# Sending four first-layer weight tiles behind the inputs of later pairs: attention with decay and a soft mixture of experts on one core

## The chip, the cores and the metric

The kernel runs on 1 core of one Trainium2 chip. The metric is the device time in microseconds (us) of one execution. In the tables and rows, PE is TensorE's matmul, PEld its weight load, DVE is VectorE, ACT is ScalarE, POOL is GpSimd and SP is SyncE, which here does nothing but issue the transfers (DMAs). The profile is of one execution; its clock starts at the first instruction.

## The reference

All data is float32. Attention with decay per head, in blocks of 64 positions, feeds a soft mixture of 8 experts with 4 slots each:

```python
# q, k, v: (4 batches, 8 heads, 768 positions, 64)
for b in range(nb):
    intra = einsum('bhic,bhjc->bhij', qb, kb) * Dmask      # lam ** (i - j), lower triangle
    intra = einsum('bhij,bhjd->bhid', intra, vb)
    inter = einsum('bhid,bhde->bhie', qb * lam_pow, kv_state)
    out[:, :, sl] = intra + inter
    kv_state = lam_block * kv_state + einsum('bhsd,bhse->bhde', kb * rev_pow, vb)
# x: the output as (3072 tokens, 512); phi: (512, 32 slots)
logits = x @ phi
slot_input = softmax over tokens(logits).T @ x              # 32 x 512
for e in range(8):                                          # w1: (8, 512, 1024), w2: (8, 1024, 512)
    slot_out[e] = maximum(slot_input[e] @ w1[e], 0) @ w2[e]
return softmax over slots(logits) @ slot_out                # 3072 x 512
```

The two weight arrays are 16.8 MB each, q, k and v together some 19 MB, the output 6.3 MB.

## The kernel before

**The pairs.** The sequence is cut into blocks of 128 positions, and two batches are worked on at a time, so there are 12 pairs, p = 0 to 11. Each pair needs three input tiles of 512 KB (k, q and v; two buffers of each). In turn p of the main loop PE computes, in this order: the part carried over from the state (`carried(p)`, matmuls a<-q,st), the part from within the block (`values(p)`, a<-at,v), the new state (`state(p)`, s<-v,kd), and then the scores of the next pair (`scores(p + 1)`, w<-q,k), after which come the logits of two pairs, the slots' sums and the transposes. Every engine keeps the order in which the program is written. DVE multiplies the scores by the mask (at<-w,mask) and updates the state (st).

**The weights.** Each layer's weights come as 32 tiles of 512 KB: w1t for the first layer, w2t for the second. 35 buffers (28 called slab, 7 called hold) take all 32 w1t tiles and the first 3 w2t tiles; the other w2t tiles go into buffers that come free as the main loop ends (those of k, q, v, kd, mask, at, xt, x) and, from there on, into slabs whose w1t tile has been used. The first layer (a<-w1t,e and w<-w1t,e) and the second (r<-w2t,hz and w<-w2t,hz) run behind the main loop, and use the tiles in the order in which they are sent for. The output is written as 24 pieces of 256 KB (y<-o), the first ten before the second layer's last part, the other 14 after it.

**The order of transfers.** All transfers are issued by SP in one order and go to one queue. SP issues a transfer as soon as the ones ahead of it have been issued and its own conditions hold: a free buffer, a PE instruction that it is kept behind, and the landing of the transfer eight places ahead of it. In turn p the inputs of pair p + 2 are sent for, k behind `carried(p)`, q behind `state(p)`, v behind `scores(p + 1)`. Between them `SENT[p]`, four numbers, says how many weight tiles are sent for at the four points of the turn: behind k, behind q, behind v, and at the end of the turn.

```python
def next_weights(p, point, at_):
    for _ in range(SENT.get(p, (0, 0, 0, 0))[point]):
        if early:
            behind(load_early(1), at_)
        elif run["spare"] < SPARE:
            run["spare"] += 1
            behind(load_late(bufs=NSLAB), at_)
```

`early` is the list of w1t tiles that are left; when it is empty, the 3 spare slabs take w2t tiles. Two w1t tiles are sent for ahead of the loop.

Of the kernel before, what the change touches and what calls it, by code (L numbers as in the profile page):

```python
# [33 lines left out]
LAST = (1, 0, 2)  # L34

SENT = {
    0: (1, 0, 1, 1), 1: (1, 0, 1, 1), 2: (1, 1, 1, 1), 3: (1, 0, 1, 1), 4: (1, 0, 1, 1), 5: (1, 1, 1, 1),
    6: (1, 1, 1, 1), 7: (1, 1, 1, 1), 8: (1, 0, 1, 1), 9: (1, 0, 1, 0),
}
NHOLD = 7  # L40

# [767 lines left out]
```

## Time and profile before

| | |
|---|---|
| median of 3 runs | 159.81 us (159.24 to 159.82) |
| the profiled execution's own time | 158.95 us |
| its span, first to last instruction | 157.1 us |
| PE busy | 142.7 us (91%) |
| DVE, ACT, POOL busy | 97.9, 50.9, 22.0 us |
| bytes moved | 59.14 MB, 376 GB/s over the span |

The span is 1.85 us less than the execution's own time; that rest lies ahead of the first instruction and behind the last one. PE's busy time says how long matmuls were under way, not that PE ran at its peak. The queue's share of busy time (99.2% on the page) counts transfers that are under way, so it is the GB/s, not the share, that tells how much was moved.

### The profile page before, as it was taken

What the parts mean: (1) busy time and instruction counts of PE and PEld (TensorE: products, weight loads), DVE (VectorE), ACT (ScalarE), POOL (GpSimd) and SP (SyncE); (2) the same over time, 40 slices, a digit from 0 to 9 for tenths busy, and PEclk for the clock granted to TensorE, in tenths of its full rate; (3) what the DMA queues carried; (4) which work ended last, traced back from release to release, by engine and by line L of the source; (5) the groups of instructions that cost most, each with busy time, mean ns of one, the idle gap of its engine ahead of it and who ended that gap; (6) DMA issues with size and microseconds to landing.
All of it is one profiled execution on the core that took longest, in us unless ns stands there. A gap on an engine that the chain in (4) does not pass through costs nothing.

```text
span 157.1 us, 5471 instructions
## 1 busy us (share of the span) xinstructions
PE 142.7 (91%) x2336; PEld 112.6 (72%) x2336; DVE 97.9 (62%) x209; ACT 50.9 (32%) x119; POOL 22.0 (14%) x35
## 2 busy tenths in 40 slices
PE   6999999999999999989999799999899999999500
PEld 6898999897897999887999679687333365756500
DVE  4699792768829473949376691955579971705800
ACT  3020225130550245021613036015037981604600
POOL 1003030303003000212030300300024840000000
PEclk9999999999999999999999999999999999999975
DMA  4999999999999999999999999899999999998995
GB/s 105 351 396 396 384 352 407 414 409 417 405 417 406 412 411 413 409 410 416 409 412 408 407 406 366 318 288 308 406 403 407 404 408 407 391 334 302 370 384 188
DMA packets 30424, 59.14 MB, mean 376 GB/s; under 512 B 2753, under 2 KB 8897, under 8 KB 30401
## 3 DMA queue, kind: packets, MB, share of 16 engines
q1 hardware_dynamic: 30400, 58.80, 99.2%
q8 instruction: 18, 0.29, 0.7%
q14 instruction: 6, 0.04, 0.1%
HBM read 52.50 MB, written 6.29 MB: 374 GB/s over the span
## 4 chain that ended last, share of the span: by engine, by line
PE 67%; DMA 21%; DVE 2%; SPq 2%; issue 1%; DVEq 0%; ACT 0%
PE a L52 26%; PE w L52 25%; DMA q<-qT 19%; PE r L52 10%; PE s L52 7%; SPq L52 2%; DMA y<-o 2%; DVE o L52 2%; DVEq L805 0%; DVE s L52 0%; ACT e L52 0%; DVE e L52 0%; DVEq L52 0%
## 5 line engine op out<-in xcount | busy, mean ns | idle before, releaser
L52 DVE TENSOR_TENSOR at<-w,mask 128x512 f32<-128x512 f32 x48 | 30.7, 681 | 6.9 <-PE w L52 6.7
L52 PE MATMUL w<-q,k 64*128 64x128 f32 x384 | 24.9, 278 | 2.5 <-DMA q<-qT 2.5
L52 PEld LDWEIGHTS w<-q,k 64*128 64x128 f32 x384 | 22.6, 188 | 4.1 <-issue 2.5
L52 POOL TENSOR_TENSOR q<-q,qpow 128x512 f32<-128x512 f32 x10 | 12.8, 1277 | 83.4 <-PE w L52 60.7
L52 PE MATMUL a<-at,v 128*64 128x128 f32 x384 | 23.6, 276 | 0.0
L52 ACT COPY xt<-a 128x512 f32<-128x512 f32 x23 | 12.4, 589 | 33.6 <-PE a L52 33.5
L52 PEld LDWEIGHTS a<-at,v 128*64 128x64 f32 x384 | 20.7, 137 | 2.1 <-issue 2.1
L52 DVE SCALAR_TENSOR_TENSOR st<-st,qpow,s 128x128 f32<-128x128 f32 x32 | 9.0, 343 | 16.9 <-PE s L52 16.9
L52 ACT COPY x<-a 128x512 f32<-128x512 f32 x12 | 6.9, 587 | 24.7 <-PE a L52 24.7
L52 DVE TENSOR_TENSOR kd<-w,mask 128x512 f32<-128x512 f32 x18 | 12.0, 683 | 1.4 <-PE w L52 1.2
L52 PE MATMUL a<-q,st 64*64 64x128 f32 x320 | 11.0, 275 | 0.0
L52 PE MATMUL s<-v,kd 128*64 128x64 f32 x320 | 11.0, 222 | 0.0
L52 PE MATMUL w<-ident,k 128*128 128x128 f32 x72 | 10.8, 279 | 0.0
L52 PEld LDWEIGHTS s<-v,kd 128*64 128x64 f32 x320 | 10.7, 138 | 0.0
L52 PEld LDWEIGHTS a<-q,st 64*64 64x64 f32 x320 | 8.6, 132 | 2.3 <-issue 1.5
L52 PEld LDWEIGHTS w<-ident,k 128*128 128x128 f32 x72 | 8.0, 140 | 1.0
L52 PE MATMUL a<-ident,xt 128*128 128x128 f32 x56 | 8.5, 280 | 0.0
L52 PEld LDWEIGHTS a<-ident,xt 128*128 128x128 f32 x56 | 6.1, 140 | 3.2 <-issue 3.1
L52 ACT CAST ct<-part 32x256 fp32r<-32x256 f32 x20 | 8.1, 402 | 0.3
L52 PE MATMUL a<-w1t,e 128*32 128x512 f32 x64 | 7.1, 594 | 0.4 <-DVE e L52 0.4
L52 PE MATMUL w<-w2t,hz 128*32 128x256 f32 x128 | 7.5, 380 | 0.0
L52 POOL CAST ct<-part 32x256 fp32r<-32x256 f32 x16 | 7.1, 445 | 2.7 <-issue 2.0
(118 smaller groups left out, 170.7 us busy)
## 6 DMA issues: line engine op xcount, KB each, us to landing
w1t<-w_x SPq DMA_DIRECT2D x32, 512.0 KB, 9.2
w2t<-w_x SPq DMA_DIRECT2D x32, 512.0 KB, 8.7
y<-o SPq DMA_DIRECT2D x24, 256.0 KB, 3.3
k<-kT SPq DMA_DIRECT2D x11, 512.0 KB, 7.6
q<-qT SPq DMA_DIRECT2D x11, 512.0 KB, 8.4
v<-vN SPq DMA_DIRECT2D x11, 512.0 KB, 8.9
k<-kT SPq DMA_DIRECT2D x2, 256.0 KB, 3.1
q<-qT SPq DMA_DIRECT2D x2, 256.0 KB, 3.5
```

The costliest lines, as they stand in the source:

```text
L52: return self._tc.keep_in_program_order(f(*args, **kwargs))
```

## The change

The numbers of `SENT` are changed, and nothing else. Four w1t tiles are no longer sent for in turns 0, 2, 5 and 7 (one each); turn 9 sends for two tiles at its end, and a new turn 10 for two behind `carried(10)` and `values(10)`.

```diff
 SENT = {
-    0: (1, 0, 1, 1), 1: (1, 0, 1, 1), 2: (1, 1, 1, 1), 3: (1, 0, 1, 1), 4: (1, 0, 1, 1), 5: (1, 1, 1, 1),
-    6: (1, 1, 1, 1), 7: (1, 1, 1, 1), 8: (1, 0, 1, 1), 9: (1, 0, 1, 0),
+    0: (1, 0, 0, 1), 1: (1, 0, 1, 1), 2: (1, 0, 1, 1), 3: (1, 0, 1, 1), 4: (1, 0, 1, 1), 5: (1, 0, 1, 1),
+    6: (1, 1, 1, 1), 7: (1, 0, 1, 1), 8: (1, 0, 1, 1), 9: (1, 0, 1, 2), 10: (2, 0, 0, 0),
 }
```

The sum of the numbers is 33 before and after (30 w1t tiles and 3 w2t tiles). The instructions of PE, DVE, ACT and POOL keep their order; SP's order alone changes. The first place is SP's order in turns 0 and 1, from v of pair 2 to v of pair 3, before:

```order
L52 DMA v_253<-vN 128x2x512
L52 DMA w1t_255<-w1_x 128x1024
L52 DMA w1t_267<-w1_x 128x1024
L52 DMA k_306<-kT 128x2x512
L52 DMA w1t_308<-w1_x 128x1024
L52 DMA q_333<-qT 128x2x512
L52 DMA v_357<-vN 128x2x512
```

And the same place after the change:

```order
L52 DMA v_253<-vN 128x2x512
L52 DMA w1t_265<-w1_x 128x1024
L52 DMA k_304<-kT 128x2x512
L52 DMA w1t_306<-w1_x 128x1024
L52 DMA q_331<-qT 128x2x512
L52 DMA v_355<-vN 128x2x512
```

One weight tile less stands ahead of pair 3's k, q and v, and ahead of all that follows. The same happens behind q of pair 4, of pair 7 and of pair 9, so that v of pair 4 has two tiles fewer ahead of it, v of pair 7 three, and v of pair 9 and all inputs of pairs 10 and 11 four.

The second place is SP's order at the end of the main loop, from the last tile of turn 8 on; k, q and v are those of pair 11. Before:

```order
L52 DMA w2t_1232<-w2_x 128x2x512
L52 DMA k_1266<-kT 128x2x512
L52 DMA w2t_1268<-w2_x 128x2x512
L52 DMA q_1293<-qT 128x2x512
L52 DMA v_1317<-vN 128x2x512
L52 DMA w2t_1319<-w2_x 128x2x512
L52 DMA w2t_1374<-w2_x 128x2x512
L52 DMA w2t_1392<-w2_x 128x2x512
L52 DMA w2t_1443<-w2_x 128x2x512
```

After the change:

```order
L52 DMA w1t_1224<-w1_x 128x1024
L52 DMA k_1258<-kT 128x2x512
L52 DMA w1t_1260<-w1_x 128x1024
L52 DMA q_1285<-qT 128x2x512
L52 DMA v_1309<-vN 128x2x512
L52 DMA w1t_1311<-w1_x 128x1024
L52 DMA w1t_1366<-w1_x 128x1024
L52 DMA w2t_1368<-w2_x 128x2x512
L52 DMA w2t_1370<-w2_x 128x2x512
L52 DMA w2t_1388<-w2_x 128x2x512
L52 DMA w2t_1416<-w2_x 128x2x512
L52 DMA w2t_1418<-w2_x 128x2x512
L52 DMA w2t_1443<-w2_x 128x2x512
```

The last two w1t tiles and all w2t tiles now stand behind pair 11's v, and four more tiles stand between that v and the w2t tile that goes into v's freed buffer (w2t_1443). From that tile on the order is the same, and the same set of tiles stands ahead of it.

## Rows read from the trace of the kernel before

**Rows 1.** The page: span, and all that the queue moved.

```profile
span 157.1 us, 5471 instructions
...
DMA packets 30424, 59.14 MB, mean 376 GB/s; under 512 B 2753, under 2 KB 8897, under 8 KB 30401
```

**Rows 2.** Groups on PE, 11.4 to 94.3 us: busy, mean ns, idle before <-releaser.

```profile
L52 PE MATMUL w<-q,k 64*128 64x128 f32 x320 | 20.6, 278 | 2.3 <-DMA q<-qT 2.2
L52 PE MATMUL a<-at,v 128*64 128x128 f32 x288 | 17.7, 276 | 0.0
```

**Rows 3.** PE's timeline: start, us, what, idle before <-releaser.

```profile
28.39 2.06 PE L52 MATMUL w<-q,k 64*128 64x128 f32 x32 [0.27 <-DMA q<-qT]
...
35.94 2.06 PE L52 MATMUL w<-q,k 64*128 64x128 f32 x32 [0.38 <-DMA q<-qT]
...
69.03 2.06 PE L52 MATMUL w<-q,k 64*128 64x128 f32 x32 [0.57 <-DMA q<-qT]
...
87.70 2.06 PE L52 MATMUL w<-q,k 64*128 64x128 f32 x32 [1.02 <-DMA q<-qT]
...
118.19 7.05 PE L52 MATMUL w<-w1t,e 128*32 128x512 f32 x64
...
136.68 5.82 PE L52 MATMUL w<-w2t,hz 128*32 128x256 f32 x104
```

**Rows 4.** The chain that ended last: start, us, what (issue to landing).

```profile
78.83 8.73 DMA q<-qT
```

**Rows 5.** Windows: PE, PEld, DVE, ACT, POOL busy (instructions), PEclk, DMA share, GB/s.

```profile
40.00:86.00 46.00, 45.40 (x827) 40.28 (x827) 29.53 (x60) 15.71 (x39) 5.11 (x4) 1.00 1.04 411
94.30:98.20 3.90, 3.90 (x98) 3.64 (x97) 0.53 (x3) 2.54 (x8) 0.00 (x0) 1.00 1.02 367
98.20:102.10 3.90, 3.90 (x48) 2.67 (x46) 3.58 (x8) 0.27 (x1) 1.28 (x1) 1.00 0.86 319
102.10:106.00 3.90, 3.90 (x85) 3.12 (x85) 2.05 (x4) 0.59 (x1) 0.00 (x0) 1.00 0.96 284
106.00:110.00 4.00, 3.75 (x57) 3.05 (x58) 2.20 (x7) 2.13 (x7) 0.00 (x0) 1.00 1.02 311
146.50:155.00 8.50, 1.10 (x9) 0.87 (x7) 2.34 (x4) 1.58 (x4) 0.00 (x0) 0.77 1.09 384
```

**Rows 6.** SP's timeline, six short windows: when single transfers were issued.

```profile
47.20 0.38 SPq L52 DMA_DIRECT2D v<-vN  x1
...
88.19 0.37 SPq L52 DMA_DIRECT2D v<-vN  x1
...
100.54 0.37 SPq L52 DMA_DIRECT2D w2t<-w_x  x1
...
102.83 0.37 SPq L52 DMA_DIRECT2D w2t<-w_x  x1
...
128.89 0.75 SPq L52 DMA_DIRECT2D w2t<-w_x  x1
...
152.24 0.58 SPq L52 DMA_DIRECT2D y<-o  x1
```

**Rows 7.** The same six transfers: KB, and us from issue to landing.

```profile
v<-vN SPq DMA_DIRECT2D x1, 512.0 KB, 6.6
...
v<-vN SPq DMA_DIRECT2D x1, 512.0 KB, 8.5
...
w2t<-w_x SPq DMA_DIRECT2D x1, 512.0 KB, 4.2
...
w2t<-w_x SPq DMA_DIRECT2D x1, 512.0 KB, 6.3
...
w2t<-w_x SPq DMA_DIRECT2D x1, 512.0 KB, 10.2
...
y<-o SPq DMA_DIRECT2D x1, 256.0 KB, 3.4
```

**Rows 8.** Tile w1t, all 32 transfers.

```profile
DMA to landing us min/median/max: 5.2/9.2/10.6
```

**Rows 9.** DVE's timeline behind the longest of PE's waits.

```profile
88.87 1.29 DVE L52 TENSOR_TENSOR at<-w,mask 128x512 f32<-128x512 f32 x2 [1.01 <-PE w L52]
```

## The prediction

> **What bounds the kernel now.** I read the page's totals first, then the groups on PE in the main loop, then PE's own timeline, and last the transfers one by one. The page gives a span of 157.1 us in which the one queue moved 59.14 MB [rows 1]. In the main loop PE is almost never idle: of all its groups there, only the scores stand behind a wait that counts, 2.3 us in all, and 2.2 of them ended when a q tile landed; the group below it, like all others, has 0.0 [rows 2]. The timeline shows where these waits are: 0.27 us ahead of pair 3's scores, 0.38 ahead of pair 4's, 0.57 ahead of pair 8's and 1.02 ahead of pair 10's [rows 3]. The chain of waits says the same from the other side: q of pair 10 is issued at 78.83 and lands 8.73 later, at 87.56, and the scores start at 87.70 [rows 3, 4]. So each late q was sent for in time, and then stood in the queue behind other tiles.
>
> The queue is the second thing to watch. From 40 to 86 us it moves 411 GB/s, so a tile of 512 KB (524,288 bytes) takes 1.28 us. From 94.3 to 110 us it moves only 367, 319, 284 and 311 GB/s [rows 5], since there the next tiles wait for buffers that PE and DVE still use. The time lost there against 411 GB/s is 3.9 x (1 - 367/411) = 0.42, then 0.87, 1.21 and, over 4.0 us, 0.97: 3.47 us. At the very end the last writes move at 384 GB/s, 0.68 us for each 256 KB [rows 5].
>
> **What the change removes.** From pair 3 on, inputs have fewer weight tiles ahead of them: one for q of pairs 3 and 4, three for q of pair 8, four for q of pair 10. In a queue that never runs dry that brings them forward by 1.28, 1.28, 3.8 and 5.1 us. PE needs them earlier by the wait itself and by what it has gained before: 0.27, then 0.38 + 0.27 = 0.65, then 1.22, then 2.24 us. Each is less than what the tile gains, so all four waits should go, and with 0.6 us or more to spare. Inputs that were in time before gain at least as many tiles, so none of them should become late. The sum of the four, 0.27 + 0.38 + 0.57 + 1.02, is **2.24 us**.
>
> Two things could keep part of it. First, the queue must not run dry: the shortest stay from issue to landing near the end of the loop, when little is queued, is 4.2 us (the transfer issued at 100.54) [rows 6, 7]. V of pair 6 now stays 6.6 us [rows 7]; with two tiles fewer ahead and issued 0.65 us earlier, that is 6.6 - 2.55 + 0.65 = 4.7. V of pair 11 stays 8.5 us [rows 7] and will stay 8.5 - 5.1 + 2.24 = 5.6. Both are above 4.2, so the queue gets short but stays filled. Second, DVE used PE's wait to catch up: behind the longest one it stood idle for 1.01 us, up to 88.87, until the scores came [rows 9]. So DVE was free from 87.86. Without the wait PE would start at 86.68 and be through the first half of the scores, which DVE waits for, 1.03 us later (half of 2.06, [rows 3]), at 87.71. DVE would then begin at most 0.15 us late, which at four places is 0.6 us if PE felt all of it; I take 0, since PE goes on to logits that do not need DVE's product, and keep 0.6 for the range.
>
> **What the change adds.** Four tiles, 5.1 us of the queue, move into the stretch with 3.47 us lost. Two w1t tiles are sent for behind all inputs; a w1t tile never took more than 10.6 us to land [rows 8], so they are there by about 101 us (my estimate: issue by 90). They are the last of the first layer and are used in the last quarter of the matmuls that start at 118.19 and take 7.05 us [rows 3], at 123.5. That costs nothing. What matters is whether w2t and the writes behind them come later, since all of them share the queue.
>
> Up to the transfer issued at 100.54 the same set of tiles has been sent for before and after. Before, it landed at 100.54 + 4.2 = 104.74 [rows 6, 7]. After: v of pair 11 landed at 88.19 + 8.5 = 96.69 and will land 5.1 us earlier, at 91.59; ten tiles then follow (six before), and 91.59 + 10 x 1.28 gives 104.4. The next transfer, issued at 102.83, landed at 102.83 + 6.3 = 109.13, which is 4.39 us behind the one ahead of it instead of 1.28 [rows 6, 7]: it goes into the mask's buffer, it was issued late, and the queue was nearly empty. After the change it is issued 2.24 us earlier, while the queue still has tiles to move. If only the issue counts, it lands at 106.9; if only the queue counts, at 105.7. So the stream of w2t tiles comes 2.2 to 3.4 us earlier, and I take 2.24.
>
> Is that enough? The last w2t tile landed at 128.89 + 10.2 = 139.09 [rows 6, 7]. PE's last part, 104 instructions of 0.056 us from 136.68 [rows 3], first touches it some 92 instructions in, at 141.8: 2.7 us to spare, so PE may run 2.24 us ahead even if that tile came no earlier. The writes are tighter. 24 of them at 0.68 us need 16.4 us; behind 139.09 that is 155.5, and the last one landed at 152.24 + 3.4 = 155.64 [rows 6, 7]. There is only 0.2 us between the two: to let the end come 2.24 us earlier, the stream has to come at least 2.0 us earlier too. The estimate above, 2.2 to 3.4, meets that with little room. The sum therefore stays at 2.24 us: the span goes from 157.1 to 154.9, the profiled execution from 158.95 to 156.7. The median of the runs shown, 159.81, lies 0.86 us above the profiled execution; taken off the median the sum gives 157.6. Should those 0.86 us be waits of the same kind, they go as well, and 156.7 is the low bound. I say 157.5.
>
> **The rivals.** The first is that the stream, not PE, sets the end. If the slow transfer at 102.83 takes its 4.39 us again although the queue is full, it lands at 104.4 + 4.39 = 108.8, the stream gains 0.4 us, and the end gains that and the 0.2 from above: 0.6 us, 159.2. For it speaks that the transfers there were slow while some were under way (DMA share 0.96 at 284 GB/s, [rows 5]); against it, that this coincides with late issues.
>
> A stronger form is that the queue bounds the whole program; since the bytes stay the same, nothing would change: 159.8. Against it stand the 3.47 us lost in four windows. The Trainium skill's "Perfetto Trace Analysis", section "Identifying the Most-Contended Engine", says to work on the most contended engine and to judge DMA by how far HBM's bandwidth is used; its section "Engine Utilization" puts a core's full share at 358 GB/s. By that figure an estimate for 59.14 MB is 165 us, more than the span, the kernel would have no slack and a new order of the same bytes would bring nothing. The trace does not agree: the core alone moved 411 GB/s for 46 us.
>
> The second rival ends slower. If the queue runs dry in the loop, once it has lost its backlog, the four tiles come on top: 5.1 us of work against at most 3.47 us of gaps leaves the stream 1.6 us late. The last w2t tile would land at 140.7, still in time for PE, but the writes would end at 140.7 + 16.4 = 157.1 instead of 155.64: 1.5 us slower, 161.3. It decides from the point where the stream is over 0.2 us late at 139.09, and becomes visible from 1.0 us. For it speaks that v of pair 6 gets within 0.5 us of the shortest stay; against it, that v of pair 11 keeps 1.4.
>
> The third is that waits merely shrink, by DVE's 0.15 us at each place or by engines of the queue that lag: 0.6 us of the gain lost, 158.2. I count it with the forecast.
>
> **How the numbers follow.** About 0.5% (0.8 us) is what a measurement of this kernel can tell from no change. Chances: the forecast with its own range of 156.7 to 158.3, 0.74; the stream late by the slow transfer, 159.2, 0.13; no change because the queue bounds all, 0.05; slower, 161.3, 0.08. Most of the second case lies within 0.5%, some of it above. So faster 0.79, same 0.14, slower 0.07. The range runs from 156.6, just below the low bound, to 159.2, so that it takes in the second case and leaves out the last two and the edges.
>
> **What would show it.** Right: no scores behind a q tile from 11 to 94 us in PE's groups; stays from issue to landing of 4 to 6 us for inputs from pair 9 on; the first layer's matmuls some 2.2 us earlier; more GB/s in the 16 us behind 92 us; the last w2t tile down by 2 us or more. Wrong: waits of PE for another input or for DVE's product; a queue below 400 GB/s ahead of 90 us; the last w2t tile at 139 or later while PE's last part is earlier, and writes that then follow each other at 0.68 us.

## The result and the profile after

The changed kernel takes 157.79 us (median of 4 runs, 156.70 to 158.92) against 159.81 (159.24 to 159.90): a ratio of 0.9883, 95% interval 0.9841 to 0.9925. Timed again beside three other kernels it took 157.76 (157.43 to 158.39) against 159.56, ratio 0.9887 (0.9846 to 0.9928). So it is faster by about 1.8 to 2.0 us.

The profiled execution took 158.19 us, with a span of 156.3 us, which is only 0.8 us less than before. It is worth reading closely, because it holds both what was gained and what was lost. First the same groups on PE as in [rows 2], in the same stretch (busy, mean ns, idle before):

```profile
L52 PE MATMUL w<-q,k 64*128 64x128 f32 x320 | 20.6, 278 | 0.5 <-DMA q<-qT 0.4
L52 PE MATMUL a<-at,v 128*64 128x128 f32 x306 | 18.9, 276 | 0.0
```

Of 2.3 us of waiting ahead of the scores 0.5 is left. PE's timeline has one wait for q where [rows 3] had four, and the marks behind it are the first layer's start and the first matmul behind the output's second split:

```profile
18.37 2.06 PE L52 MATMUL w<-q,k 64*128 64x128 f32 x32
...
68.09 2.06 PE L52 MATMUL w<-q,k 64*128 64x128 f32 x32 [0.45 <-DMA q<-qT]
...
109.21 1.92 PE L52 MATMUL a<-w1t,e 128*32 128x512 f32 x16 [0.44 <-DVE e L52]
...
142.35 0.74 PE L52 MATMUL a<-s,ct 128*128 128x256 f32 x4 [0.21 <-DVE s L52]
```

The same marks in the kernel before:

```profile
18.43 2.06 PE L52 MATMUL w<-q,k 64*128 64x128 f32 x32
...
111.24 1.92 PE L52 MATMUL a<-w1t,e 128*32 128x512 f32 x16 [0.44 <-DVE e L52]
...
144.38 0.74 PE L52 MATMUL a<-s,ct 128*128 128x256 f32 x4 [0.21 <-DVE s L52]
```

PE is 2.03 us earlier at both later marks, and yet the span lost only 0.8. The windows show where the queue worked (columns as in [rows 5]):

```profile
40.00:86.00 46.00, 45.46 (x840) 40.33 (x840) 28.92 (x60) 15.78 (x39) 5.10 (x4) 1.00 1.01 391
94.30:98.20 3.90, 3.90 (x84) 3.71 (x79) 1.71 (x5) 1.34 (x3) 0.45 (x1) 1.00 1.01 380
98.20:102.10 3.90, 3.90 (x69) 2.60 (x67) 3.23 (x6) 0.00 (x0) 0.83 (x1) 1.00 1.05 408
102.10:106.00 3.90, 3.90 (x63) 2.92 (x58) 1.37 (x4) 1.55 (x4) 0.00 (x0) 1.00 1.05 402
106.00:110.00 4.00, 3.31 (x58) 2.23 (x61) 2.69 (x9) 1.16 (x5) 0.00 (x0) 1.00 1.05 406
...
40.00:58.00 18.00, 18.00 (x314) 15.68 (x314) 11.17 (x24) 6.98 (x17) 1.28 (x1) 1.00 0.97 367
```

The lean windows behind 94 us are filled, as forecast: 380, 408, 402 and 406 GB/s in place of 367, 319, 284 and 311. But a new lean stretch stands in the main loop, 367 GB/s from 40 to 58 us, where PE is busy all the time. Single transfers, first as issued by SP (start, us): v of pair 6 and the weight tile behind it, v of pair 11, the counterpart of the slow transfer issued at 102.83 before [rows 6], the last w2t tile and the last write.

```profile
46.36 0.38 SPq L52 DMA_DIRECT2D v<-vN  x1
...
47.25 0.34 SPq L52 DMA_DIRECT2D w1t<-w_x  x1
...
86.19 0.38 SPq L52 DMA_DIRECT2D v<-vN  x1
...
100.80 0.37 SPq L52 DMA_DIRECT2D w2t<-w_x  x1
...
128.24 0.75 SPq L52 DMA_DIRECT2D w2t<-w_x  x1
...
150.30 0.56 SPq L52 DMA_DIRECT2D y<-o  x1
```

And the same six with the time from issue to landing in the last column:

```profile
v<-vN SPq DMA_DIRECT2D x1, 512.0 KB, 4.6
...
w1t<-w_x SPq DMA_DIRECT2D x1, 512.0 KB, 6.6
...
v<-vN SPq DMA_DIRECT2D x1, 512.0 KB, 7.1
...
w2t<-w_x SPq DMA_DIRECT2D x1, 512.0 KB, 6.9
...
w2t<-w_x SPq DMA_DIRECT2D x1, 512.0 KB, 10.2
...
y<-o SPq DMA_DIRECT2D x1, 256.0 KB, 4.6
```

V of pair 6 stays 4.6 us in the queue (6.6 before, [rows 7]) and lands at 51.0; the weight tile right behind it lands at 53.9, so this tile took 2.9 us of the queue instead of 1.28. The last w2t tile lands at 138.4, 0.6 us earlier than before, not 2. The 24 writes need 16.4 us behind it, which gives 154.8, and the last one lands at 154.9: here the stream, not PE, sets the end.

### The profile page after: what moved, and what is told of

It reads as the page before. It is cut to its first block, busy times and chain, and to the rows that moved or that the text cites. A ratio compares the mean times of both kernels' runs of the same rounds, so it can differ in the third digit from the quotient of the medians.

```text
span 156.3 us, 5474 instructions
## 1 busy us (share of the span) xinstructions
PE 142.7 (91%) x2336; PEld 112.8 (72%) x2336; DVE 97.6 (62%) x209; ACT 50.9 (33%) x119; POOL 22.0 (14%) x35
## 4 chain that ended last, share of the span: by engine, by line
PE 84%; DMA 5%; DVE 2%; issue 1%; DVEq 0%; ACT 0%
PE w L52 33%; PE a L52 30%; PE s L52 12%; PE r L52 10%; DMA q<-qT 5%; DVE o L52 1%; DVEq L805 0%; DVE s L52 0%; DVE warm L52 0%; ACT so L52 0%; ACT e L52 0%; DVE e L52 0%; DVE so L52 0%; DVEq L52 0%
```

## Experiments

The theory: the gain is that inputs land earlier because fewer weight tiles stand ahead of them, and the end is the later of two times, PE's and the stream's. The main rival: the gain comes from filling the lean windows behind 94 us. In each, only what the diff shows is changed; SP's order alone moves, unless it says otherwise.

**One tile, turn 0 alone.**

```diff
-    0: (1, 0, 1, 1),  ...  9: (1, 0, 1, 0),
+    0: (1, 0, 0, 1),  ...  9: (1, 0, 1, 1),
```

> One tile only leaves its place (turn 0) and is sent for in turn 9, so every later input has one tile, 1.28 us, less ahead of it. If the gain is that inputs land earlier (my theory): the waits at pairs 3, 4 and 8 (0.27, 0.38, 0.57) go, at pair 10 about 0.96 us is left (2.24 needed, 1.28 given), gain 1.28 us against the kernel before, 158.5. If the gain comes from the four tiles filling the lean windows behind 94 us (rival), one tile gives a quarter of the 2.0 measured: 0.5 us, 159.3.

Measured: 157.98 us, ratio 0.9914 (0.9880 to 0.9947), 1.4 us faster. This fits the theory's 1.28 us; a quarter of the gain, 0.5 us, lies outside the interval. The profiled execution, with 159.12 us one of the slower ones of 12, shows the waits that stay, at pairs 8 and 10:

```profile
69.00 2.06 PE L52 MATMUL w<-q,k 64*128 64x128 f32 x32 [0.64 <-DMA q<-qT]
...
87.90 2.06 PE L52 MATMUL w<-q,k 64*128 64x128 f32 x32 [1.25 <-DMA q<-qT]
```

Pairs 3 and 4 wait no more, as expected; pair 8 still waits, which I had not expected, and pair 10 waits 1.25 instead of 0.96. This execution lies 1.1 us above the median, and in it PE gained only 0.6 us from pair 2's scores to the first layer, so the 1.4 us rests on the medians and not on this trace. One tile ahead of pair 10's q, issued at 76.08, landed 2.5 us behind the tile before it (82.8 to 85.3) instead of 1.28. Such delays differ from one execution to the next: the kernel of the third experiment below, whose transfers have the same order as before up to the last four w2t tiles, waits 0.20 us ahead of pair 4, 0.91 ahead of pair 8, 1.04 ahead of pair 10 and not at all ahead of pair 3, where [rows 3] have 0.38, 0.57, 1.02 and 0.27.

**Two tiles, turns 5 and 7 alone.**

```diff
-    5: (1, 1, 1, 1),  ...  7: (1, 1, 1, 1),  ...  9: (1, 0, 1, 0),
+    5: (1, 0, 1, 1),  ...  7: (1, 0, 1, 1),  ...  9: (1, 0, 1, 2),
```

> Two tiles leave their places (turns 5 and 7). My theory: the waits at pairs 3 and 4 (0.27 and 0.38) stay, those at pairs 8 and 10 (0.57 and 1.02) go, since one and two tiles give 1.28 and 2.55 us; gain 1.6 us, 158.2; and the queue keeps its length from 40 to 58 us, where the changed kernel's ran short, so that the last w2t tile should land earlier than the changed kernel's 138.45. Rival (tiles fill the lean windows): half of the gain, 1.0 us, 158.8.

Measured: 157.53 us, ratio 0.9871 (0.9825 to 0.9918): 1.9 to 2.1 us faster, as much as the four tiles gave. The rival's 1.0 us lies outside the interval, the theory's 1.6 inside. The waits at pairs 3 and 4 stay, and those at pairs 8 and 10 are gone:

```profile
28.78 2.06 PE L52 MATMUL w<-q,k 64*128 64x128 f32 x32 [0.69 <-DMA q<-qT]
...
36.79 2.06 PE L52 MATMUL w<-q,k 64*128 64x128 f32 x32 [0.84 <-DMA q<-qT]
```

Both are longer in this execution than before (0.27 and 0.38), so a wait of one profile is not a fixed size. The queue keeps its rate from 40 to 58 us, 410 GB/s, since nothing was taken out ahead of that stretch, and the last w2t tile lands at 126.44 + 10.3 = 136.7. PE is later than in the changed kernel, the stream earlier, and the sum is no worse.

**The stream shortened at its end, in the kernel before and in the changed one.**

```diff
         Q, f, i = late.pop()
+        if len(late) < 4:
+            for y in range(2):
+                wt["w2", Q, 2 * i + y, f] = wt["w2", 1, y, 5]
+            return None
```

> The kernel before, without the transfers of the last four w2t tiles (the second layer's last part uses one earlier tile in their place, so the output's last part is not the reference's); PE's work is the same. The stream is 5.1 us shorter. If PE sets the end of the kernel before, as I read it, it stays within 0.4 us of it: 159.4 to 159.8. If the stream sets it, up to 5 us faster.

> The changed kernel without the transfers of the last four w2t tiles (same omission). If the stream sets the end of the changed kernel, as its profile reads (writes back to back from 138.45 on), it is faster than the changed kernel by what PE is ahead, 0.5 to 1.5 us, so 2.2 to 2.6 us faster than before in all: 156.5 to 157.3, with less spread from run to run. If PE alone sets the end, it equals the changed kernel, 157.8.

Measured: before, 159.42 us against 159.45, ratio 0.9994 (0.9966 to 1.0023); changed, 156.96 us, ratio 0.9834 (0.9790 to 0.9877), from 156.71 to 157.47. Taking 5.1 us of transfers away does nothing for the kernel before: PE sets its end. A stream that comes earlier can therefore not have been the gain, as the rival would have it. In the changed kernel the same omission brings the time from 157.8 to 157.0, with a range of 0.8 us instead of 2.2 and 1.0. The two intervals overlap, so the 0.8 us by itself is not certain; that the writes of the changed kernel's profile end where the stream's sum says, and not where PE's does, is the firmer sign. The changed kernel's profile without the four tiles has no wait for q behind the start, and its rate from 40 to 58 us is 384 GB/s.

**Only the order within a turn.**

```diff
-    0: (1, 0, 1, 1), 1: (1, 0, 1, 1), 2: (1, 1, 1, 1),  ...  9: (1, 0, 1, 0),
+    0: (0, 0, 2, 1), 1: (0, 0, 2, 1), 2: (0, 0, 3, 1),  ...  9: (0, 0, 2, 0),
```

> No tile leaves its turn: the weight tiles of a turn that stood behind k or q are sent for behind v, so that each q has one tile, 1.28 us, less of its own turn's weights ahead of it and the queue keeps its length. My theory (a q that lands earlier is the gain): as in the run that moves turn 0's tile alone, gain 1.3 us, 158.2. Rival (the tiles must leave the main loop): no change, 159.5.

Measured: 158.75 us, ratio 0.9929 (0.9896 to 0.9962). It is a gain of 0.8 to 1.1 us, less than the 1.3 expected (the interval reaches from 0.6 to 1.7), but no tile left the main loop, so the rival is wrong that the tiles must leave it. The profiled execution waits 0.62 us for pair 10's q, and in the main loop for no other.

**Three tiles, so that the queue keeps one more from turn 2 on.**

```diff
-    2: (1, 0, 1, 1),  ...  10: (2, 0, 0, 0),
+    2: (1, 1, 1, 1),  ...  10: (1, 0, 0, 0),
```

(The lines taken away are those of the changed kernel.)

> Three tiles leave their places (turns 0, 5 and 7); turn 2 keeps its fourth, so that the queue from 40 to 58 us is a tile longer than in the changed kernel, where the transfers ran thin and the stream lost time. My theory (both PE's waits and the stream matter): no q wait of over 0.3 us, the stream at 400 GB/s or more from 40 to 58 us, the last w2t tile below 138, 157.2, some 0.5 us faster than the changed kernel. Rival (the order of the stream has no part in the end): as the changed kernel, 157.8.

Measured: 157.34 us (156.54 to 158.05), ratio 0.9847 (0.9807 to 0.9888). It beats the kernel before, and stands 0.4 us below the changed one, which the intervals do not separate. The spans set them further apart: 154.3 to 155.8 us here against 155.6 to 156.5 for the changed kernel timed beside it, medians 155.05 and 155.9. The executions with three, with two and with eight tiles are each 2.2 to 2.3 us longer than their spans, those of all other kernels 1.8 to 1.9; what the 0.4 us outside the span are, no run shows. The profile with three tiles has the lowest span of all, 154.3 us, and no wait for q at all behind the start. The window from 40 to 58 us:

```profile
40.00:58.00 18.00, 18.00 (x312) 15.68 (x312) 11.34 (x24) 6.98 (x17) 1.27 (x1) 1.00 1.03 403
```

403 GB/s where the changed kernel had 367, with one tile more in the queue; the last w2t tile lands at 125.93 + 10.2 = 136.1. PE's marks:

```profile
18.58 2.06 PE L52 MATMUL w<-q,k 64*128 64x128 f32 x32
...
108.78 1.92 PE L52 MATMUL a<-w1t,e 128*32 128x512 f32 x16 [0.44 <-DVE e L52]
...
141.92 0.74 PE L52 MATMUL a<-s,ct 128*128 128x256 f32 x4 [0.21 <-DVE s L52]
```

**Eight tiles** (the lines taken away are again those of the changed kernel).

```diff
-    0: (1, 0, 0, 1), 1: (1, 0, 1, 1), 2: (1, 0, 1, 1),  ...  5: (1, 0, 1, 1),  ...  7: (1, 0, 1, 1),  ...  10: (2, 0, 0, 0),
+    0: (1, 0, 0, 1), 1: (1, 0, 0, 1), 2: (1, 0, 0, 1),  ...  5: (1, 0, 0, 1),  ...  7: (1, 0, 0, 1),  ...  10: (6, 0, 0, 0),
```

> Eight tiles leave the main loop instead of four. My theory: PE has no q waits left to lose, the queue runs dry within the loop (below 390 GB/s from 40 to 86 us), and the stream comes late: the last w2t tile at 142 or later, and the writes behind it end 16.4 us later; 161 to 163, slower than before. Rival (more tiles behind the inputs are better, the lean windows behind 94 us take them): 157 to 158.

Measured: 162.25 us, ratio 1.0161 (1.0123 to 1.0199), slower, as the theory says and near its number. The rate from 40 to 58 us (361 GB/s from 40 to 86), then PE's waits for transfers (us in total, times, longest), those for w2t in the second layer, that for q ahead of pair 1's scores:

```profile
40.00:58.00 18.00, 18.00 (x312) 15.69 (x311) 11.37 (x23) 6.94 (x16) 1.28 (x1) 1.00 0.94 347
```

```profile
PE w L52 <- DMA w2t<-w_x: 2.1, 4, 0.7
...
PE w L52 <- DMA q<-qT: 0.2, 1, 0.2
```

The last w2t tile lands at 132.47 + 10.5 = 143.0; 16.4 us more make 159.4, and the last write lands at 153.98 + 5.36 = 159.3.

**The changed kernel again.**

> The changed kernel once more, on the same chip as the three others. 157.8 (156.7 to 158.9). If the loss of the stream from 47 to 58 us in its first profile comes from the short queue, it is there again (below 390 GB/s from 40 to 58 us); if it was a chance event, the stream moves 405 GB/s or more there.

Measured: 157.76 us, as above. The lean stretch is there again, while no q is waited for behind the start:

```profile
40.00:58.00 18.00, 18.00 (x311) 15.85 (x310) 11.37 (x23) 6.65 (x16) 1.28 (x1) 1.00 1.01 374
```

And PE's marks:

```profile
19.06 2.06 PE L52 MATMUL w<-q,k 64*128 64x128 f32 x32
...
109.26 1.92 PE L52 MATMUL a<-w1t,e 128*32 128x512 f32 x16 [0.45 <-DVE e L52]
...
142.39 0.74 PE L52 MATMUL a<-s,ct 128*128 128x256 f32 x4 [0.21 <-DVE s L52]
```

## Why the prediction was right, and where a step failed

The time was forecast as 157.5 us and is 157.8. Two terms were off, PE's gain too small and the stream's too large, and they nearly cancel; that the time came within 0.3 us is in part luck. Of the signs of being wrong that were named ahead one came true, a queue below 400 GB/s ahead of 90 us (391 from 40 to 86 us); and of the signs of being right the stays of 4 to 6 us were missed (v of pair 11 stayed 7.1 us in the first profile and 6.2 in the second).

**What bounds the kernel before: right.** PE sets its end and the queue does not; with 5.1 us fewer transfers it took the same time. This also speaks against the stronger form of the first rival, in which the queue bounds everything. The 358 GB/s in the Trainium skill, "Perfetto Trace Analysis", section "Engine Utilization", was no bound here: the core moved 411 GB/s. The same section says that 358 is the share of a core when both cores of a pair use the memory, and that one core alone can go to some 120% of it; the trace agrees, with 115%. The estimate of 165 us left that condition out.

**The four waits: right, but mis-sized.** They go when the q tiles have fewer weight tiles ahead of them: one tile moved gave 1.4 us, and the new order within a turn a part. All four are gone in the changed kernel's second profile, while the first keeps 0.45 us ahead of pair 8. The term was 2.24 us, the sum of four idle times. From pair 2's scores to the first layer PE took 111.24 - 18.43 = 92.81 us before; in the changed kernel's second profile 109.26 - 19.06 = 90.20, and with three tiles moved 108.78 - 18.58 = 90.20 as well. So without the waits PE was 2.61 us earlier. PE's timeline counts a wait from the modelled end of the last matmul to the next start; the starts themselves lie further apart than that. Pair 10's scores start 87.70 - 79.52 = 8.18 us behind pair 9's before and 85.67 - 78.58 = 7.09 after, 1.09 for a wait of 1.02. The four places make 2.5 us in this way; the last 0.1 lies between pairs 5 and 6, where no q was waited for.

**"The queue gets short but stays filled": failed.** The stay of v of pair 6 came out as worked out, 4.6 for 4.7 us. But the sign was badly chosen: a stay above 4.2 us does not mean that the queue moves all it can. The transfer that stayed 4.2 us belongs to a stretch with 319 and 284 GB/s [rows 5, 6, 7], and it was not the shortest either, since the one issued at 98.30 stayed 4.0. What goes with the rate is the number of tiles under way. The fewest tiles that were issued and had not landed at any moment from 44 to 50 us, and the rate of these 6 us, in all ten profiles:

| fewest tiles under way | profiles | GB/s |
|---|---|---|
| 5 | before; before without four w2t tiles | 411, 411 |
| 4 | one tile; two; three; order within a turn | 396, 413, 398, 401 |
| 3 | changed; changed again; changed without four w2t tiles | 346, 313, 349 |
| 2 | eight tiles | 304 |

The rate from 40 to 58 us follows the number of tiles taken out ahead of pair 6's v: none, 410 GB/s (two tiles moved, in turns 5 and 7); one, 402 and 403 (turn 0 alone; three tiles); two, 367, 374 and 384 (the changed kernel twice, and without four w2t tiles); four, 347 (eight tiles). The tile that took 2.9 us in the first profile is not the cause: in the second it landed 1.2 us behind pair 6's v, and the stretch was lean all the same. Why three tiles under way do not fill the queue is not settled. The second rival, a queue that runs dry in the loop, so had the mechanism right, but with four tiles the loss was smaller than what PE gained; with eight it came out as that rival said.

**The stream 2.2 to 3.4 us earlier: failed.** Most of it follows from the step before: from 40 to 58 us the first profile lost 18 x (1 - 367/411) = 1.9 us of the stream. V of pair 11 landed at 86.19 + 7.1 = 93.3 and not at 91.59. The slow transfer that the first rival feared did not come back, since its counterpart, issued at 100.80, landed 1.3 us behind the tile ahead of it, with 402 to 408 GB/s around it. But it landed at 107.7, 2.0 us later than the 105.7 that the queue's sum gave, and so 1.4 earlier than before. One tile issued at 104.14 then landed 2.6 us behind the one ahead (111.6 to 114.2), for a reason that no run shows. The last w2t tile came at 138.4 in the first profile and at 127.47 + 10.2 = 137.7 in the second, so 0.6 and 1.4 us earlier, less than the 2.0 that the prediction had asked for. So the first rival named the right end, the stream, and the wrong place.

**The end as the later of two times: right.** The stream's sum is the landing of the last w2t tile and 16.4 us for 24 writes at 0.68 us. PE's sum is the start of the matmul behind the second split and 11.26 us (155.64 - 144.38, taken from the kernel before, which is therefore no test). The last write should land at the later of the two (all in us):

| profile | stream's sum | PE's sum | last write landed |
|---|---|---|---|
| one tile | 155.8 | 155.8 | 155.9 |
| two tiles | 153.1 | 154.7 | 154.7 |
| three tiles | 152.5 | 153.2 | 153.2 |
| changed | 154.8 | 153.6 | 154.9 |
| changed again | 154.1 | 153.7 | 154.1 |
| eight tiles | 159.4 | 157.2 | 159.3 |
| order within a turn | 153.8 | 154.2 | 154.7 |
| before, without four w2t tiles | 148.7 | 155.4 | 155.9 |
| changed, without four w2t tiles | 149.4 | 153.9 | 154.2 |

Six agree within 0.1 us. The last three end 0.3 to 0.5 us later than the later sum; what was late there is not shown. In the changed kernel's first profile the stream cost 1.3 us beyond PE's sum and 0.4 to 0.5 in the second. That is the difference between the full gain and what was measured.

**First-layer weights, DVE.** Neither cost anything: no wait of PE for w1t, and without waits for q PE takes the same 90.20 us in four profiles (changed again, changed without four w2t tiles, three tiles, eight tiles), so DVE's late start, for which up to 0.6 us was kept in the range, did not show.

## What to carry to other kernels

When an input lands late in a shared queue, count what stands ahead of it: each 512 KB tile taken out brings it forward by up to its own 1.28 us (pair 10's q, with four out, landed at 84.4 in place of 87.6, 3.2 us earlier and not 5.1), and what the compute engine gained at earlier waits has to be covered too. Work out the end as the later of the compute chain and the transfers still to come, and move no more out of the queue than the waits need, since time lost in a queue that runs short comes back at the end. Count the tiles under way where the queue is shortest: here four or more held 396 GB/s or more, and three did not. The same change with eight tiles was 1.6% slower, with two or three at least as fast as with four.

## What was not expected of the hardware

With one queue and tiles of 512 KB, the rate fell by 6 to 10% (410 to 367, 374 and 384 GB/s over 18 us) although three tiles or more were under way all the time from 44 to 50 us, where it was lowest, and a tile stayed 4.6 us from issue to landing, 3.6 times the 1.28 us that it takes at full rate. And executions of one kernel differ before the change can act: pair 2's scores began at 18.37 us in one profile of the changed kernel and at 19.06 in another, 0.69 us apart, where the runs of one kernel lie 1.0 to 2.2 us apart.
